# Unit 4's output products in three parts, unit 6's transposes before unit 5's scores, three weight sums moved, and all kept outputs stored ahead of unit 10's transposes

## The chip, the cores and the metric

The kernel runs on one NeuronCore of a Trainium2 chip. A time is the device time of one execution in microseconds (us). The kernel before was run three times: 223.66, 223.75 and 224.96 us, median 223.75. One further execution was taken with the hardware profiler; every duration quoted comes from it.

The core has five engines that run their own instruction streams and wait for each other by semaphores: TensorE (PE, its weight loads shown as PEld), VectorE (DVE), ScalarE (ACT), GpSimd (POOL) and SyncE (SP, which here only issues DMAs).

## What is computed

A linear-attention layer with decay, followed by a bilinear feed-forward layer. For each of 4 batches and 8 heads (sequence 768, head size 64), in blocks:

```
intra  = (q k^T * Dmask) v            Dmask[i,j] = lam^(i-j) for i >= j, else 0
inter  = (q * lam^(i+1)) kv_state
out    = intra + inter
kv_state = lam^block * kv_state + (k * lam^(block-1-j))^T v
```

The attention output, with heads side by side, is x with 3072 rows of 512. The feed-forward part has weights w_a, w_b (512 x 1536) and w_out (1536 x 512):

```
out = ((x @ w_a) * (x @ w_b)) @ w_out
```

Inputs and output are float32; the products are made in bfloat16 with float32 sums.

## The kernel before, in words

A **unit** is 128 rows of one batch for all 8 heads; there are 24, six in each batch. For a unit, q, k and v (256 KB each) are loaded by SyncE into rotating buffers (three of each, line 187). GpSimd scales k and q by powers of lam to bfloat16 (prep_k, line 401; VectorE for the first k's), and one of three engines casts v (prep_v, line 420). For units 7 to 23 SyncE then issues a transposing DMA of the scaled pair (line 429, tile qkT); for units 4 to 6 TensorE transposes it by matmuls ("T", line 443) and ScalarE copies the result (line 445). "S" makes the scores (line 457) and VectorE masks them (line 480); "V" updates the kv state (line 527) and copies it (line 560); "O" or "O2" adds inter and intra products (line 497) for one or two units and ScalarE brings the result out as xT (line 520), which is the feed-forward part's input.

The feed-forward part runs over **groups** of 4, 1, 2, 4, 4, 4, 4 and 1 units: group 0 is units 0 to 3, group 1 is unit 4 alone, group 2 is units 5 and 6, group 3 is units 7 to 10. Groups 0, 1, 2 and 7 use plain products (function ffn): for each of the 12 slices f of the inner size, a_ps and b_ps (line 596), ScalarE's cast of a_ps to a_sb (line 605) and VectorE's product ab (line 623); then per unit 12 output products op (line 643) and a store. Groups 3 to 6 (function ffn_z) use a scheme of seven products instead of eight (line 748), for which sums of the weights are made beforehand: **weight sums** 0 to 7 (function weight_sum, lines 269 to 275; even ones of w_a, odd ones of w_b; sums 6 and 7 are wz_a[3] and wz_b[3], used by the fifth product of each slice). In these groups ScalarE copies intermediate PSUM banks to tiles u of a pool of 7 buffers (snap, line 829).

**Order of the work.** Attention pieces for later units are put between the feed-forward products by hand. PLAN lists, for each group, pairs of a slot and a piece; hook(slot) issues the pieces of that slot. In ffn, slot f comes behind slice f. After the 12 slices come, for each unit t, half of the output products, slot 12 + 2t, the other half, the store, slot 13 + 2t. Within an engine the instructions run in this order; engines only wait for each other's data and buffers. Loads are issued by pump(), called at the end of prep_v and limited by a look-ahead of one to three units.

**Kept outputs.** The outputs of units 0 to 4 are copied by ScalarE (line 634) into tiles o_kept of the snap pool and not stored at once; each "W" in PLAN issues one store (store_kept, line 629), so five snap buffers stay taken until these stores have landed. Later outputs are stored at once (line 639).

All loads, transposing DMAs and stores stand in SyncE's one queue, in the order of the program. Around the change it is: transpose 7; loads of unit 10; transpose 8; kept stores 1 and 2; transposes 9 and 10; loads of units 11 and 12; transpose 11; loads of unit 13; kept store 3; transpose 12; loads of unit 14; an output; transpose 13; loads of unit 15; kept store 4; an output; kept store 5; transpose 14.

The PSUM has 7 banks in rotation for these tiles (ps_bank); a tile that comes seven later waits until the bank's reader is done.

Of the kernel before, what the change touches and what calls it, by code (L numbers as in the profile page):

```python
# [22 lines left out]
def _bc(ap, dims):  # L23
# [81 lines left out]
                        ["act"] * 3))  # L105
SUM_ENG = {(3, 0): 'dve', (3, 1): 'dve', (3, 2): 'pool', (3, 3): 'dve', (3, 4): 'pool', (3, 5): 'pool', (3, 6): 'dve', (3, 7): 'dve', (4, 0): 'dve', (4, 1): 'pool', (4, 2): 'pool', (4, 3): 'pool', (4, 4): 'dve', (4, 5): 'pool', (4, 6): 'pool', (4, 7): 'pool', (5, 0): 'dve', (5, 1): 'dve', (5, 2): 'pool', (5, 3): 'pool', (5, 4): 'dve', (5, 5): 'pool', (5, 6): 'pool', (5, 7): 'dve', (6, 0): 'pool', (6, 1): 'dve', (6, 2): 'pool', (6, 3): 'dve', (6, 4): 'dve', (6, 5): 'pool', (6, 6): 'dve', (6, 7): 'dve'}
XS_ENG = {(3, 0): 'dve', (3, 1): 'dve', (3, 2): 'dve', (4, 0): 'dve', (4, 1): 'dve', (4, 2): 'dve', (5, 0): 'dve', (5, 1): 'pool', (5, 2): 'pool', (6, 0): 'pool', (6, 1): 'pool', (6, 2): 'pool'}
WS_ENG = {0: 'dve', 1: 'dve', 2: 'dve', 3: 'dve', 4: 'dve', 5: 'dve', 6: 'dve', 7: 'pool'}
WO_ENG = {0: 'dve', 1: 'dve', 2: 'pool', 3: 'dve', 4: 'dve'}
CO_ENG = {0: 'pool', 1: 'pool', 2: 'pool', 3: 'dve', 4: 'dve', 5: 'dve'}  # L110

# [2 lines left out]
def kernel(  # L114
# [12 lines left out]
    B, H, S, D = q.shape  # L127
# [3 lines left out]
    d_model, d_ff = moe_w_a.shape  # L131
# [4 lines left out]
    FC = d_ff // 128  # L136
# [202 lines left out]
    for w, src in (("q", q), ("k", k)):  # L339
# [3 lines left out]
        for c in range(0, HP, n_c):  # L343
# [4 lines left out]
            t = t[:].rearrange("p (c b x) -> p c b x", c=n_c, b=2)  # L348
# [282 lines left out]
    def store(row, op, lo, hi, queue=None):  # L631
        if row < g_u0[KEEP_GROUPS]:
            o_sb = snap_pool.tile([128, d_model], F32, name="o_kept", tag="snap")
            nc.scalar.copy(o_sb, op)
            kept.append((row, o_sb))
            return
        o_sb = o_pool.tile([128, d_model], F32, name="o_sb", tag="osb")
        nc.scalar.copy(o_sb[:, lo:hi], op[:, lo:hi])
        (queue or nc.sync).dma_start(out=out_r[row][:, lo:hi], in_=o_sb[:, lo:hi])

    def out_mms(op, ab, t, fs, lo=0, hi=d_model):
        for f in fs:
            nc.tensor.matmul(op[:, lo:hi], lhsT=ab[:, f, t * 128:(t + 1) * 128],  # L643
                             rhs=wo_sb[:, f, lo:hi], start=(f == 0), stop=(f == FC - 1))

    def ffn(u0, n, xT, hook, first, last):
        gt = n * BLK
        ab = ab_pool.tile([128, FC, 512], BF16, name="ab", tag="ab")
        if first:
            for i, cs in enumerate(W_STEPS):  # L650
                nxt = W_STEPS[i + 1] if i + 1 < len(W_STEPS) else ()
                fs = range(w_off[cs[0]] // 128, w_off[cs[-1] + 1] // 128)
                a_sbs = a_parts(fs[:2], xT, gt) if i == 0 else []
                a_sbs += [a_part(f, xT, gt) for f in fs[len(a_sbs):]]
                if i == 0:
                    kv_update(n0 - 1)
                    cast_w("b", cs[1], "both")
                else:
                    for c in nxt:
                        cast_w("a", c, "dve")  # L660
                for n_f, (f, a_sb) in enumerate(zip(fs, a_sbs)):
                    b_part(f, xT, gt, a_sb, ab)
                    hook(f)
                    if i == 0 and n_f == 1:
                        cast_w("a", nxt[0], "dve")
                for c in nxt:
                    cast_w("b", c, "act")
            ops = [ps_bank("op", [128, d_model], F32, hold=True) for _ in range(n)]
            slot = FC
            for c in range(FC // 2):  # L670
                for t in range(n):
                    out_mms(ops[t], ab, t, range(2 * c, 2 * c + 2))
                    if c == FC // 2 - 1:
                        store(u0 + t, ops[t], 0, d_model)
                    hook(slot)
                    slot += 1
            bank["held"].clear()
            return
        for f in range(FC):
            a_sb = a_part(f, xT, gt)  # L680
            b_part(f, xT, gt, a_sb, ab)
            hook(f)
        for t in range(n):
            op = ps_bank("op", [128, d_model], F32, ffn=True)
            if last and t == n - 1:
                for lo, hi in ((0, 256), (256, 384), (384, 512)):
                    if lo:
                        op = ps_bank("op", [128, d_model], F32, ffn=True)
                    out_mms(op, ab, t, range(FC), lo, hi)
                    store(u0 + t, op, lo, hi, nc.scalar if hi == d_model else None)  # L690
                return
            out_mms(op, ab, t, range(FC // 2))
            hook(FC + 2 * t)
            out_mms(op, ab, t, range(FC // 2, FC))
            store(u0 + t, op, 0, d_model)
            hook(FC + 2 * t + 1)
# [318 lines left out]
    for g, n in enumerate(GROUPS):  # L1015
# [6 lines left out]
        def hook(slot, plan=plan):  # L1022
            for name, us in plan.get(slot, ()):
                if name == "C":
                    cast_w("o", us, CO_ENG[us])
                elif name == "PK":
                    prep_k(us)
                elif name == "PV":
                    prep_v(us)
                elif name == "P":  # L1030
                    prep_k(us)
                    prep_v(us)
                elif name == "W":
                    store_kept()
                elif name == "WS":
                    weight_sum(us)
                elif name == "WO":
                    out_sum(us)
                elif name == "SM":
                    ab_sum(*us)  # L1040
                elif name == "H":
                    out_half(*us)
                elif name == "XA":
                    x_add_first(us)
                elif name == "X":
                    x_sums(us)
                elif name == "T":
                    piece_T(us)
                elif name == "S":
                    piece_S(us)  # L1050
                elif name == "VC":
                    kv_copy(us, kv["ps"], KV_ENG[us])
                elif name == "V":
                    piece_V(us)
                elif name == "O":
                    pieces_O((us,))
                elif name == "O2":
                    pieces_O(us)
                else:
                    pieces_O(us[:2], us[2:])  # L1060
# [41 lines left out]
```

## Time and profile before

| what | value |
|---|---|
| median of three runs | 223.75 us |
| the profiled execution | 223.83 us, of which 222.1 us are the span from the first to the last instruction |
| TensorE busy | 213.9 us (96%) |
| VectorE, ScalarE, GpSimd busy | 165.3, 122.7, 99.8 us |
| bytes moved | 39.4 MB, mean 177 GB/s |
| unit 4's output products | 58.3 to 61.5 us |
| group 2's slices | 62.8 to 74.5 us |
| group 3 begins | 83.0 us |

How to read it. Times in lists are microseconds from the start of the span. A row of a timeline has the start, the duration of the whole row (several instructions may be merged, x says how many), the engine, the line, the operation, out<-in, shapes and, in brackets, how long the engine had been idle and what ended that. "SPq" rows are SyncE issuing a DMA: their duration is that of the issue, and the transfer lands some microseconds later. Matmuls are pipelined, so a busy TensorE says only that something was in its pipe; gaps are found from the distance of one matmul's start to the next. An idle time of an engine that is not the bottleneck costs nothing by itself.

### The profile page before, as it was taken

The numbers are of one execution on the slowest core, as the hardware profiler recorded it, in microseconds if no ns is written. First come the engines' busy times: TensorE is split into PE (matmuls) and PEld (weight loads), VectorE is DVE, ScalarE is ACT, GpSimd is POOL, SyncE is SP. The second block draws the span as 40 slices with busy tenths as digits, with TensorE's granted clock in tenths as the row PEclk, the third lists the DMA queues.
The fourth block names the chain that finished last, engine by engine and source line by source line (L and its number), as shares of the span: only waits on it lengthen the run. The fifth ranks groups of instructions, "written<-read, shape, count | busy, mean of one in ns | idle before, by whom it ended". The sixth has DMA issues, their size and how long they took to land.

```text
span 222.1 us, 5601 instructions
## 1 busy us (share of the span) xinstructions
PE 213.9 (96%) x2225; PEld 159.0 (72%) x2235; DVE 165.3 (74%) x272; ACT 122.7 (55%) x249; POOL 99.8 (45%) x95
## 2 busy tenths in 40 slices
PE   7899999999999999999999999899999999999994
PEld 2476444448678657787547888688888888888994
DVE  0994773968798668889888889968688865777540
ACT  3686446038454266775356988776535666543322
POOL 6061004246795175540559559786417722051100
PEclk9999999999999999999999999999999999999999
DMA  4999999999999999999999999652021100112042
GB/s 132 321 265 349 356 387 344 277 216 218 216 204 220 232 174 248 190 275 245 180 248 236 233 201 211 138 101 50 0 88 56 52 0 4 47 47 97 0 145 94
DMA packets 99081, 39.42 MB, mean 177 GB/s; under 512 B 85488, under 2 KB 95088, under 8 KB 99056
## 3 DMA queue, kind: packets, MB, share of 16 engines
q1 hardware_dynamic: 98768, 39.00, 79.8%
q8 instruction: 17, 0.28, 0.6%
q10 hardware_dynamic: 288, 0.07, 0.1%
q14 instruction: 8, 0.07, 0.1%
HBM read 28.32 MB, written 6.29 MB: 156 GB/s over the span
## 4 chain that ended last, share of the span: by engine, by line
PE 67%; DMA 16%; SPq 5%; DVE 5%; ACT 2%; issue 2%; POOL 1%; ACTq 0%; DVEq 0%; POOLq 0%
PE U L748 17%; PE op L870 12%; PE V L748 9%; DMA wst<-in_moe_w_b_dram 8%; PE b_ps L596 5%; PE op L810 5%; PE a_ps L596 5%; PE W L748 4%; PE op L643 3%; DMA kf<-in_k_dram 3%; DMA k<-in_k_dram 3%; PE o_ps L497 3%; PE kq L457 2%; DMA out_dram<-o_kept 2%; SPq L187 1%
## 5 line engine op out<-in xcount | busy, mean ns | idle before, releaser
L829 ACT COPY u<-U 128x512 f32<-128x512 f32 x48 | 28.3, 590 | 16.5 <-PE U L748 16.4
L401 POOL TENSOR_TENSOR qk<-kf,lp_k 128x512 bf16<-128x512 f32 x18 | 19.5, 1084 | 33.7 <-DMA kf<-in_k_dram 18.9
L623 DVE TENSOR_TENSOR ab<-a_sb,b_ps 128x128 bf16<-128x128 bf16 (+2 forms) x48 | 19.2, 417 | 13.6 <-ACT a_sb L605 10.2
L596 PE MATMUL a_ps<-xT,wa_sb 128*128 128x128 bf16 (+2 forms) x198 | 27.6, 267 | 0.5 <-DVE wa_sb L244 0.2
L480 DVE TENSOR_TENSOR m<-kq,lotri 128x512 bf16<-128x512 f32 x40 | 25.6, 682 | 3.1 <-PE kq L457 3.0
L596 PE MATMUL b_ps<-xT,wb_sb 128*128 128x128 bf16 (+2 forms) x192 | 27.5, 272 | 0.2
L756 DVE TENSOR_TENSOR ab<-oab 128x1024 bf16<-128x1024 bf16 x24 | 19.0, 791 | 11.3 <-ACT oab L754 11.1
L401 POOL TENSOR_TENSOR qk<-qf,lp_q 128x512 bf16<-128x512 f32 x20 | 24.8, 1242 | 1.7 <-DMA qf<-in_q_dram 1.7
L605 ACT CAST a_sb<-a_ps 128x128 bf16<-128x128 f32 (+2 forms) x48 | 17.3, 374 | 14.7 <-PE a_ps L596 14.4
L643 PE MATMUL op<-wo_sb,ab 128*128 128x512 bf16 (+2 forms) x114 | 21.8, 334 | 0.5 <-issue 0.3
L596 PEld LDWEIGHTS <-wa_sb 128*128 128x128 bf16 x200 | 16.7, 98 | 6.6 <-issue 0.5
L748 PEld LDWEIGHTS <-wz_a 128*128 128x128 bf16 x192 | 18.2, 98 | 3.9 <-issue 0.9
L748 PEld LDWEIGHTS <-wz_b 128*128 128x128 bf16 x192 | 18.7, 98 | 2.2
L596 PEld LDWEIGHTS <-wb_sb 128*128 128x128 bf16 x192 | 15.8, 98 | 6.2 <-issue 0.2
L748 PE MATMUL U<-xT,wz_a 128*128 128x256 bf16 x96 | 18.3, 272 | 0.0
L748 PE MATMUL U<-xT,wz_b 128*128 128x256 bf16 x96 | 18.3, 272 | 0.0
L520 ACT CAST xT<-o_ps 128x512 bf16<-128x512 f32 (+1 forms) x24 | 12.2, 554 | 10.7 <-PE o_ps L497 10.5
L787 DVE TENSOR_TENSOR oab<-U,u 128x512 bf16<-128x512 f32 x24 | 16.3, 681 | 0.8 <-PE U L748 0.8
L420 POOL CAST vb<-vf 128x512 bf16<-128x512 f32 x14 | 10.2, 730 | 13.8 <-DMA vf<-in_v_dram 13.8
L748 PEld LDWEIGHTS <-wa_sb 128*128 128x128 bf16 x144 | 13.4, 98 | 4.0 <-issue 1.0
L643 PEld LDWEIGHTS <-ab 128*128 128x128 bf16 x120 | 10.1, 98 | 8.5
L754 ACT CAST oab<-U 128x512 bf16<-128x512 f32 x24 | 14.2, 592 | 3.5 <-PE U L748 3.5
(130 smaller groups left out, 453.1 us busy)
## 6 DMA issues: line engine op xcount, KB each, us to landing
vf<-in_v_dram SPq DMA_DIRECT2D x24, 256.0 KB, 4.9
qf<-in_q_dram SPq DMA_DIRECT2D x20, 256.0 KB, 4.6
kf<-in_k_dram SPq DMA_DIRECT2D x20, 256.0 KB, 4.7
out_dram<-o_sb SPq DMA_DIRECT2D x18, 256.0 KB, 2.4
wst<-in_moe_w_a_dram SPq DMA_DIRECT2D x6, 512.0 KB, 8.8
wst<-in_moe_w_b_dram SPq DMA_DIRECT2D x6, 512.0 KB, 9.2
wst<-in_moe_w_out_dram SPq DMA_DIRECT2D x6, 512.0 KB, 10.7
out_dram<-o_kept SPq DMA_DIRECT2D x5, 256.0 KB, 4.3
```

The costliest lines, as they stand in the source:

```text
L401: eng_of(eng).tensor_mul(dst.rearrange("p (c b) d -> p b c d", b=2), x[:].rearrange("p (b c) d -> p b c d", b=2), lp.rearrange("p (b c) o ...
L480: nc.vector.tensor_mul(m, kq[i], lotri_bc)
L596: nc.tensor.matmul(ps[:, lo:hi], lhsT=w_sb[:, s, f * 128:(f + 1) * 128], rhs=xT[:, s, lo:hi], start=(s == 0), stop=(s == KS - 1), skip_gro ...
L605: nc.scalar.copy(a_sb[:, :gt], ps[:, :gt])
L623: nc.vector.tensor_mul(ab[:, f, :gt], a_sb[:, :gt], ps[:, :gt])
L643: nc.tensor.matmul(op[:, lo:hi], lhsT=ab[:, f, t * 128:(t + 1) * 128], rhs=wo_sb[:, f, lo:hi], start=(f == 0), stop=(f == FC - 1))
L748: nc.tensor.matmul(ps[:, k, :], lhsT=wt[:, s, n * 128:(n + 1) * 128], rhs=rhs[i][:, s, :], start=(fresh and k == 0 and s == 0), stop=True, ...
L754: nc.scalar.copy(oab[:, 0], U)
L756: nc.vector.tensor_mul(ab[:].rearrange("p (h i) (t c) -> p h i t c", h=2, t=2)[:, :, n], o5[:, :, :, 0, :], o5[:, :, :, 1, :])
L787: nc.vector.tensor_sub(oab[:, 1], U, v1)
L829: nc.scalar.copy(t, ps)
L870: nc.tensor.matmul(ps[:, t, :], lhsT=lhs[p][:, n, t * 128:(t + 1) * 128], rhs=rhs[:, n, :], start=fresh, stop=True, skip_group_check=True)
```

## The change

Four things are edited.

1. Unit 4's output products (the branch n == 1 of ffn, which only group 1 takes): 4 products, slot 12, 4 products, slot 13, 4 products, store. Before: 6 products, slot 12, 6 products, store, slot 13. So the pieces of slot 13 (preparation of unit 8, O2 of units 5 and 6, V of unit 6 and a weight sum) stand ahead of the last 4 products, and ScalarE's copy of unit 4's output behind its copies of xT.
2. At slot 11 of group 1, T of unit 6 comes before S of unit 5.
3. Weight sum 5 goes from slot 0 to slot 13 of group 1. Sum 6 goes from slot 13 of group 1 to slot 9 of group 2. Sum 7 goes from slot 13 of group 1 to slot 13 of group 2, and from GpSimd to VectorE. VectorE has one instruction more, GpSimd one less.
4. The kept stores: three at slot 2 of group 2 (before: two), two at slot 6 (before: one each at slots 11, 13 and 15). In SyncE's queue, store 3 now stands ahead of transpose 9 and stores 4 and 5 between transposes 9 and 10; the later places are empty. The number of DMAs is the same.

TensorE has the same instructions. Its order changes only at unit 5's scores and unit 6's transposes, and in the place of the output products of unit 4.

```diff
-    1: [(0, 'PV', 5), (0, 'WS', 5), (3, 'T', 5), (4, 'PK', 6), (6, 'PV', 6), (9, 'P', 7),
-        (11, 'S', 5), (11, 'T', 6), (12, 'S', 6), (13, 'P', 8), (13, 'O2', (5, 6)), (13, 'V', 6),
-        (13, 'WS', 6), (13, 'WS', 7)],
-    2: [(2, 'W', None), (2, 'W', None), (3, 'P', 9), (4, 'V', 7), (4, 'S', 7),
-        (6, 'V', 8), (10, 'PK', 10), (11, 'PV', 10), (11, 'P', 11), (11, 'W', None),
+    1: [(0, 'PV', 5), (3, 'T', 5), (4, 'PK', 6), (6, 'PV', 6), (9, 'P', 7),
+        (11, 'T', 6), (11, 'S', 5), (12, 'S', 6), (13, 'P', 8), (13, 'O2', (5, 6)), (13, 'V', 6), (13, 'WS', 5)],
+    2: [(2, 'W', None), (2, 'W', None), (2, 'W', None), (3, 'P', 9), (4, 'V', 7), (4, 'S', 7),
+        (6, 'V', 8), (6, 'W', None), (6, 'W', None), (9, 'WS', 6), (10, 'PK', 10), (11, 'PV', 10), (11, 'P', 11),
         (11, 'S', 8), (11, 'P', 12), (12, 'Q', (7, 8, 9, 10)), (13, 'P', 13),
-        (13, 'W', None), (13, 'V', 9), (14, 'XA', 3), (14, 'O2', (9, 10)), (14, 'X', 3), (15, 'W', None)],
+        (13, 'V', 9), (13, 'WS', 7), (14, 'XA', 3), (14, 'O2', (9, 10)), (14, 'X', 3)],
...
-WS_ENG = {0: 'dve', 1: 'dve', 2: 'dve', 3: 'dve', 4: 'dve', 5: 'dve', 6: 'dve', 7: 'pool'}
+WS_ENG = {0: 'dve', 1: 'dve', 2: 'dve', 3: 'dve', 4: 'dve', 5: 'dve', 6: 'dve', 7: 'dve'}
...
+            if n == 1:
+                out_mms(op, ab, t, range(4))
+                hook(FC)
+                out_mms(op, ab, t, range(4, 8))
+                hook(FC + 1)
+                out_mms(op, ab, t, range(8, FC))
+                store(u0 + t, op, 0, d_model)
+                return
             out_mms(op, ab, t, range(FC // 2))
             hook(FC + 2 * t)
             out_mms(op, ab, t, range(FC // 2, FC))
```

## The prediction

> **What bounds the kernel.** First the page: the share of each engine, then the clock and DMA rows.
>
> ```profile
> PE 213.9 (96%) x2225; PEld 159.0 (72%) x2235; DVE 165.3 (74%) x272; ACT 122.7 (55%) x249; POOL 99.8 (45%) x95
> ...
> PEclk9999999999999999999999999999999999999999
> DMA  4999999999999999999999999652021100112042
> ```
>
> TensorE is busy 96% of the span at full clock, so its work sets the time and the only prize is a gap in it. The DMA engines are full until slice 25 (139 us), so in the stretch of the change (51 to 97 us) a transfer put forward puts others back. Second, the TensorE timeline, compared with an even stream: between 51 and 97 us I find four real gaps. At 54.13 us 0.27 us; at 62.80 and 63.29 us 0.29 and 0.27; at 88.75 us 0.51 (start-to-start excess over the 0.11 us of a 256-column matmul). Excesses of about 0.22 us elsewhere are a 512-column matmul missing from the trace (groups of 5 where 6 were issued). Together 1.34 us, 0.6% of the span: the change can win no more. Third, the timelines of the engines that end these gaps:
>
> ```profile
> 52.48 1.39 DVE L273 TENSOR_TENSOR wz_b<-wb_sb,wz_b 128x1536 bf16<-128x1536 bf16 x1
> 53.80 0.67 DVE L623 TENSOR_TENSOR ab<-a_sb,b_ps 128x128 bf16<-128x128 bf16 x3
> ...
> 61.39 2.70 DVE L420 CAST vb<-vf 128x512 bf16<-128x512 f32 x1
> ```
> ```profile
> 61.58 0.58 ACT L634 COPY o_kept<-op 128x512 f32<-128x512 f32 x1 [2.01 <-PE op L643]
> 62.17 1.07 ACT L520 CAST xT<-o_ps 128x512 bf16<-128x512 f32 x2
> ```
> ```profile
> 84.85 0.40 PE L457 MATMUL kq<-qkT 64*128 64x128 bf16 x8
> ...
> 88.75 0.38 PE L748 MATMUL V<-z_add,wz_a 128*128 128x256 bf16 x2 [0.34 <-ACT u L829]
> ```
>
> Weight sum 5 holds VectorE for 1.39 us, the products behind it start at 53.80, and their PSUM banks come free late: gap one. ScalarE copies unit 4's output before it brings xT out, and the next group needs xT: gaps two and three. Before 88.75 ScalarE's copy u had waited 0.8 us for the landing of the third kept store (the only wait on such a store in the list of waits), whose buffer it reuses: gap four.
>
> Fourth, SyncE's queue and GpSimd, since transposes are issued there:
>
> ```profile
> 67.21 1.35 SPq L629 DMA_DIRECT2D out_dram<-o_kept  x2
> 68.74 3.20 SPq L429 DMA_TRANSPOSE qkT<-qk  x2
> 72.00 0.57 SPq L187 DMA_DIRECT2D qf<-in_q_dram  x1
> 72.62 0.58 SPq L187 DMA_DIRECT2D kf<-in_k_dram  x1
> ...
> 79.26 2.08 SPq L429 DMA_TRANSPOSE qkT<-qk  x1
> ...
> 83.72 1.03 SPq L629 DMA_DIRECT2D out_dram<-o_kept  x1
> ```
> ```profile
> 53.02 1.75 POOL L401 TENSOR_TENSOR qk<-qf,lp_q 128x512 bf16<-128x512 f32 x1
> ...
> 60.71 3.09 POOL L275 TENSOR_TENSOR wz_b<-wb_sb 128x1536 bf16<-128x1536 bf16 x1
> ...
> 77.19 1.04 POOL L401 TENSOR_TENSOR qk<-kf,lp_k 128x512 bf16<-128x512 f32 x1 [6.84 <-PE o_ps L497]
> 78.19 1.04 POOL L401 TENSOR_TENSOR qk<-qf,lp_q 128x512 bf16<-128x512 f32 x1
> ```
>
> SyncE issues without a pause from 60 to 78 us. Unit 11's k load is issued at 72.62 and lands 4.41 us later, at 77.03; GpSimd scales it 0.16 us after that (the releaser printed is another semaphore of the same moment), then q to 79.2; the transpose of unit 11 goes out at 79.26, takes 4.96 us, lands at 84.22, and TensorE reads it in the score matmuls at 84.85. This chain has 84.85 - 84.22 - 0.15 = **0.48 us to spare**. Unit 12's transpose lands at 89.0 for scores at 89.77; units 9, 10, 13 and 14 have 2 us or more.
>
> **The change, part by part**, against the profiled execution's 223.83 us (span 222.1; median of the runs 223.75, so the same).
>
> 1. Weight sum 5 from slot 0 of group 1 to its end: gap one goes, -0.27. At its new place (VectorE after unit 6's state copy) it takes the place of sum 6, same shape (0.95 to 1.39 against 1.19), in front of group 2's first product. Cover: the cast in front of it loses GpSimd's neighbour (part 3), so VectorE arrives earlier than before.
> 2. Unit 6's transposes (8) before unit 5's scores (8), output products 4+4+4. ScalarE's copy of the transposes takes 1.01 us (58.56) and unit 6's scores wait for it. Between the two stood 6 matmuls of 0.22 = 1.31 us; now 8 score matmuls (0.33) and 4 products (0.87) = 1.20, against 0.22 + 1.01 + 0.17 = 1.40 needed: +0.2. At the end the copy of xT no longer stands behind the copy of the output, and 4 products (0.87 us) lie between xT's source and its first reader: -0.56. The output copy now stands before group 2's first a_sb copy and frees the bank of its second a_ps at about the moment it is wanted: 0 to +0.1. Parts 1 and 2 together: **-0.66**.
> 3. Sum 7 from GpSimd (3.09 us) to VectorE at slot 13 of group 2 (0.95), sum 6 to slot 9. Sum 6 fits in VectorE's four pauses of 0.45 us per product there. Sum 7 falls at about 79.5, ahead of z_add (80.06), in the 1.6 us in which VectorE waits for xT: 0 on VectorE. Its cost is on GpSimd: beside sum 5 the q scaling took 1.75 us instead of 1.04, beside sum 6 again 1.75. Delayed as in part 4, unit 11's q scaling runs about 79.6 to 80.7, on top of sum 7. Bounds 0 and +0.95 (all of sum 7); I take the row, +0.71, in the chain that has 0.48 to spare. Freeing GpSimd at 60.7 brings unit 9 forward, which nothing waits for.
> 4. Kept stores 3, 4, 5 from after unit 13's and 15's loads to before unit 9's transpose (one) and unit 10's (two): on SyncE ahead of two transposes and the loads of units 11 and 12. Issuing one costs 0.36 to 0.49 us plus 0.06 between (the 67.21 pair), three 1.25 to 1.65; in landings, each spaces the queue by 0.64 to 0.72, three 2.0, less a pause of 0.7 (unit 10's transpose landed at 73.96, q of unit 11 1.86 later, where loads follow each other at 1.17). Both ways k of unit 11 is **1.25 to 1.65 later; I take 1.45**. Bounds: 0 (all in pauses) and 3.3 (three at 1.03 + 0.06, as the third was held at 83.72). Gap four goes, -0.51, as all kept stores land by 76 us.
>
> At unit 11's scores: its transpose is issued at 79.26 + 1.45 + 0.71 = 81.42. Its latency is 4.96 in place, 4.2 for units 8 and 12; I take 4.6: landing 86.02, scores 86.17. TensorE, early by 0.66, would be there at 84.2 and waits 2 us, with all of group 3 queued behind; parts 1 and 2 are swallowed whole. Against 84.85 that is +1.32. From there -0.51 for gap four; unit 12's transpose, no longer behind a store, lands near 90.05, before its scores at 90.1 to 90.6. Sum: +0.81, **224.6 us**. Own range: with 1.25, no neighbour, 4.2 it is 223.3; with 1.65, 0.95, 4.96 it is 225.4.
>
> The Trainium skill, "SBUF — State Buffer", section "Who interferes with whom", makes the port that VectorE and GpSimd share an exclusive lock: of a VectorE operation with two SBUF inputs and a GpSimd one that reads, the second fully blocks. The 2.70 us cast (0.56 at 57.06) agrees: it ends 0.3 us after GpSimd's 3.09 us operation. It speaks against part 3; its result is rival three.
> The Trainium skill, "DMA: Bandwidth & Descriptors", section "Queues, rings and completion order", says that each DMA engine takes one queue's descriptors in ring order, which speaks against part 4; the landings come in order of issue here too, and by it the 2.0 us would be paid except for pauses.
>
> **Rivals.**
> - *The gain is kept* (0.23). The stores fill pauses: before the first kept store landed there was a pause too (2.15 us after unit 8's transpose, 1.5 more than a store's spacing). With 0 delay and no neighbour, unit 11 lands at 84.22, scores 84.37: -0.48 - 0.51 = **222.8**; with the neighbour 223.5. Against: SyncE itself has no pause there.
> - *Slower for good* (0.12). SyncE is held 1.09 us by each of the three stores: 3.3 us, scores at 87.67: +2.82 - 0.51 = **226.1**. The change loses as soon as the chain is over 1.0 us late. For: the store at 83.72. Against: the pair at 67.21.
> - *Full blocking* (0.10). The q scaling of unit 11 stands behind sum 7 and z_add, 0.95 + 0.41 = 1.36 instead of 0.71: **225.3**. For: the cast of 2.70. Against: sum 5 and its neighbour both went on, longer.
> - *The store's wait stays* (0.05): the buffer at 88.1 is held by another user; +0.51, **225.1**.
> - Forecast: 0.50.
>
> **Numbers.** 1% (2.2 us: 221.6 and 226.1) is about what a measurement of this kernel tells from no change. Faster by more needs more than all gaps: 0.02. Slower by more: half of the second rival and a tail of the forecast, 0.08. The range 222.6 to 226.0 goes from the kept gain to that bound.
>
> **What the profile will show.** Right: no gaps at 54 and 62 to 63, group 2 some 0.7 us earlier; the cast of 2.70 back at 0.5; unit 11's k load issued at 73.3 to 73.7; a q scaling near 1.75 beside sum 7; TensorE waiting 1 to 2 us for unit 11's transpose; no wait of u on a kept store. Wrong: if unit 11's scores start before 84.85, the stores were free; if unit 12's scores wait as well, the loss is larger.

## The result

The changed kernel took 225.53 us (median of 18 runs, 223.93 to 227.68), the kernel before, beside it on the same chip, 224.14 us (18 runs, 223.41 to 225.45). The ratio, **1.0043 with a 95% interval of 1.0022 to 1.0064**, leaves out disturbed runs and so is less than that of the two medians: slower by 0.96 us on 224.14 (0.5 to 1.4), which is clear of zero and within the 1% that the prediction took as no change. The forecast was 224.6 us against 223.83; 223.75 times the ratio is 224.7.

The profiled execution of the changed kernel took 225.28 us (span 223.6). Its start-up, in which nothing was changed, was 0.32 us longer: unit 4's scores start at 48.36 us, against 48.04 before. Times of after are therefore compared with before less 0.32. A DMA has landed when its semaphore says so in the trace. Line numbers of after are one lower from L48 on, and 7 higher in ffn_z and behind it (L748 and L829 of before are L755 and L836).

The shares of the engines, from the page of after:

```profile
PE 213.7 (96%) x2225; PEld 159.0 (71%) x2235; DVE 164.3 (73%) x273; ACT 122.6 (55%) x249; POOL 96.1 (43%) x94
```

TensorE's work is the same; the difference lies in its gaps. Its timeline, the scores of units 10 to 12 (columns as in the lists above):

```profile
76.60 0.40 PE L456 MATMUL kq<-qkT 64*128 64x128 bf16 x8 [0.39 <-DMA qkT<-qk]
...
85.75 0.40 PE L456 MATMUL kq<-qkT 64*128 64x128 bf16 x8 [0.73 <-DMA qkT<-qk]
90.68 0.40 PE L456 MATMUL kq<-qkT 64*128 64x128 bf16 x8 [0.49 <-DMA qkT<-qk]
```

All four gaps of before are gone, and three new ones stand in their place, each a wait for a transpose at scores: unit 10's at 76.60, unit 11's at 85.75, unit 12's at 90.68. Start to start they cost 0.55, 0.89 and 0.66 us. Ahead of them the gain can still be seen: unit 7's scores, in the middle of group 2, start at 67.31, which less the 0.32 is 0.77 us sooner than before (67.76).

VectorE's timeline, where before had the sum of 1.39 us and the cast of 2.70 us:

```profile
61.34 0.43 DVE L419 CAST vb<-vf 128x512 bf16<-128x512 f32 x1 [0.20 <-DMA vf<-in_v_dram]
...
62.56 0.95 DVE L272 TENSOR_TENSOR wz_b<-wb_sb,wz_b 128x1536 bf16<-128x1536 bf16 x1
...
72.84 0.95 DVE L274 TENSOR_TENSOR wz_a<-wa_sb 128x1536 bf16<-128x1536 bf16 x1
...
80.18 1.83 DVE L274 TENSOR_TENSOR wz_b<-wb_sb 128x1536 bf16<-128x1536 bf16 x1
```

Sums 5 and 6 take 0.95 us, the cast 0.43. Sum 7, at 80.18, takes 1.83. GpSimd's timeline beside it:

```profile
79.15 1.04 POOL L400 TENSOR_TENSOR qk<-kf,lp_k 128x512 bf16<-128x512 f32 x1 [8.42 <-DMA kf<-in_k_dram]
80.15 1.04 POOL L400 TENSOR_TENSOR qk<-qf,lp_q 128x512 bf16<-128x512 f32 x1
81.14 1.34 POOL L419 CAST vb<-vf 128x512 bf16<-128x512 f32 x1
```

Unit 11's q scaling (80.15) took its usual 1.04 us, not the 1.75 that the prediction gave it: the price of the meeting fell on sum 7. ScalarE's timeline, where the copy of unit 4's output stood ahead of xT:

```profile
61.41 1.07 ACT L519 CAST xT<-o_ps 128x512 bf16<-128x512 f32 x2 [2.17 <-PE o_ps L496]
62.82 0.59 ACT L633 COPY o_kept<-op 128x512 f32<-128x512 f32 x1 [0.34 <-PE op L642]
```

xT now comes first. SyncE's queue, in the stretch of the stores:

```profile
67.43 1.84 SPq L628 DMA_DIRECT2D out_dram<-o_kept  x3
69.45 1.70 SPq L428 DMA_TRANSPOSE qkT<-qk  x1
71.20 1.05 SPq L628 DMA_DIRECT2D out_dram<-o_kept  x2
72.36 1.34 SPq L428 DMA_TRANSPOSE qkT<-qk  x1
73.75 0.57 SPq L186 DMA_DIRECT2D qf<-in_q_dram  x1
74.37 0.86 SPq L186 DMA_DIRECT2D kf<-in_k_dram  x1
...
81.22 2.38 SPq L428 DMA_TRANSPOSE qkT<-qk  x1
```

Unit 11's k load is issued at 74.37 (72.62 before, so 1.43 later) and lands at 78.99 (77.03, so 1.64 later). Unit 12's k load, two loads further back, lands at 83.86 instead of 80.58: 2.96 later. The chain of waits, followed to unit 12's scores, shows it as the longest piece (the last experiment asks whether this chain is what held the transpose):

```profile
77.41 6.45 DMA kf<-in_k_dram
...
84.02 0.85 POOL qk L400
...
85.02 1.04 POOL qk L400
86.06 0.40 POOL vb L419
86.47 4.16 DMA qkT<-qk
...
90.68 0.40 PE kq L456 x8
```

From unit 11's scores on, the change stays 0.58 to 0.69 us behind (unit 14's scores 105.06 against 104.05, less 0.32: 0.69), and so at the last scores. The other 0.45 us or so by which this one execution is longer lies behind the last matmul, in a stretch that differs from 3.14 to 3.62 us between the profiles of all kernels here.

### The profile page after: what moved, and what is told of

It reads as the page before. It is cut to its first block, busy times and chain, and to the rows that moved or that the text cites. A ratio compares the mean times of both kernels' runs of the same rounds, so it can differ in the third digit from the quotient of the medians.

```text
span 223.6 us, 5597 instructions
## 1 busy us (share of the span) xinstructions
PE 213.7 (96%) x2225; PEld 159.0 (71%) x2235; DVE 164.3 (73%) x273; ACT 122.6 (55%) x249; POOL 96.1 (43%) x94
## 4 chain that ended last, share of the span: by engine, by line
PE 78%; DMA 11%; DVE 4%; SPq 2%; POOL 1%; issue 1%; ACT 1%; DVEq 0%; ACTq 0%; POOLq 0%
PE U L755 17%; PE op L877 12%; PE b_ps L595 10%; PE a_ps L595 9%; PE V L755 9%; DMA kf<-in_k_dram 6%; PE op L817 5%; PE W L755 4%; PE o_ps L496 4%; PE op L642 3%; DMA k<-in_k_dram 3%; PE kq L456 2%; DMA qkT<-qk 2%; PE kvd L526 2%; SPq L349 1%; DVE m L479 1%
## 5 line engine op out<-in xcount | busy, mean ns | idle before, releaser
L836 ACT COPY u<-U 128x512 f32<-128x512 f32 x48 | 28.3, 590 | 17.0 <-PE U L755 16.9
L400 POOL TENSOR_TENSOR qk<-qf,lp_q 128x512 bf16<-128x512 f32 x20 | 23.4, 1169 | 1.6 <-DMA qf<-in_q_dram 1.6
L755 PEld LDWEIGHTS <-wz_a 128*128 128x128 bf16 x192 | 18.2, 98 | 3.4 <-issue 0.2
L755 PEld LDWEIGHTS <-wz_b 128*128 128x128 bf16 x192 | 18.8, 98 | 2.2
L755 PE MATMUL U<-xT,wz_a 128*128 128x256 bf16 x96 | 18.3, 272 | 0.0
L755 PE MATMUL U<-xT,wz_b 128*128 128x256 bf16 x96 | 18.3, 272 | 0.0
L755 PEld LDWEIGHTS <-wa_sb 128*128 128x128 bf16 x144 | 13.5, 98 | 4.0 <-issue 1.0
```

The source lines that it names most:

```text
L400: eng_of(eng).tensor_mul(dst.rearrange("p (c b) d -> p b c d", b=2), x[:].rearrange("p (b c) d -> p b c d", b=2), lp.rearrange("p (b c) o ...
L755: nc.tensor.matmul(ps[:, k, :], lhsT=wt[:, s, n * 128:(n + 1) * 128], rhs=rhs[i][:, s, :], start=(fresh and k == 0 and s == 0), stop=True, ...
L836: nc.scalar.copy(t, ps)
```

## The experiments

All but "part 4 alone" keep parts 1 to 3 and differ from the change in the stores or in one other thing. The table gives the ratio to the kernel before with its interval, and from the profiled execution the distance from unit 7's to unit 14's scores (parts 1 to 3 lie ahead of it, the stores in it; 36.29 us in before) and the gaps of TensorE in that distance that end with a transpose or a kept store, start to start.

| kernel | ratio | unit 7 to 14 | gaps |
|---|---|---|---|
| stores 3 to 5 left out | 0.996 [0.994, 0.998] | 36.04 | unit 12: 0.30 |
| late stores, q first | 0.9976 [0.995, 1.0002] | 36.29 | unit 12: 0.65 |
| stores 4, 5 at group 3, slot 11 | 0.998 [0.9959, 1.0] | 36.48 | unit 12: 0.83 |
| stores 4, 5 at group 3, slot 15 | 0.9997 [0.9974, 1.0019] | 36.66 | unit 12: 1.02 |
| only store 3 early | 1.0019 [0.9994, 1.0044] | 36.76 | unit 12: 0.31; store 4: 0.76 |
| part 4 undone | 0.9994 [0.9971, 1.0018] | 37.07 | unit 11: 0.27; store 3: 1.12 |
| stores 4, 5 at slot 12 | 1.0028 [1.0001, 1.0054] | 37.21 | unit 12: 0.65; store 4: 0.63 |
| part 4 alone | 1.0071 [1.0044, 1.0097] | 37.54 | units 11, 12: 0.89, 0.77 |
| sum 7 at slot 9 | 1.0045 [1.0016, 1.0073] | 37.58 | units 10, 11, 12: 0.43, 0.88, 0.63 |
| the change | 1.0043 [1.0022, 1.0064] | 37.75 | units 10, 11, 12: 0.55, 0.89, 0.66 |
| five stores first | 1.0056 [1.0028, 1.0084] | 38.29 | units 10, 11, 12: 0.60, 0.85, 0.90 |
| stores 4, 5 by ScalarE | 1.0033 [1.0007, 1.0058] | 38.47 | units 10, 11, 12: 1.53, 0.47, 0.67 |
| the change, q first | 1.0255 [1.0217, 1.0294] | 38.50 | units 10, 11: 0.60, 1.74; and see there |

### Part 4 undone

```diff
-    2: [(2, 'W', None), (2, 'W', None), (2, 'W', None), (3, 'P', 9), ...
-        (6, 'V', 8), (6, 'W', None), (6, 'W', None), (9, 'WS', 6), ... (11, 'P', 11),
+    2: [(2, 'W', None), (2, 'W', None), (3, 'P', 9), ...
+        (6, 'V', 8), (9, 'WS', 6), ... (11, 'P', 11), (11, 'W', None),
...
+        (13, 'W', None), (13, 'V', 9), ... (15, 'W', None)],
```

> The changed kernel with part 4 undone: the kept stores stand where the kernel before has them, parts 1 to 3 stay. Theory (the stores ahead of unit 11's loads make the loss): unit 11's transpose lands near 84.2 us again, TensorE is there at about the same moment and waits 0 to 0.3 us; the wait for the third kept store comes back, at the same absolute time (88.0 us), and so is longer than before (0.9 to 1.0 us instead of 0.51). Parts 1 and 2 show in the trace as group 2 starting 0.7 us earlier and are lost at that wait: the time is that of the kernel before, within 0.3 us (ratio 0.998 to 1.002). Rival (the new order in group 1 or the sums on VectorE make the loss): it stays slow, ratio near 1.004.

Ratio 0.9994 [0.9971, 1.0018]: parts 1 to 3 alone are worth nothing that can be measured. They bring TensorE to group 3 sooner, but the third store is where it was, so ScalarE's copy u waits longer for it (ScalarE's timeline of this kernel):

```profile
89.14 0.58 ACT L836 COPY u<-V 128x512 f32<-128x512 f32 x1 [1.44 <-DMA out_dram<-o_kept]
```

1.44 us instead of 0.83, and TensorE's gap behind it is 1.12 instead of 0.51. Most of the gain is given back at the next thing that a DMA sets: less the start-up this kernel is 1.08 us ahead of before at unit 7's scores and 0.30 at unit 12's.

### Part 4 alone

```diff
 # the kernel before, with
+    2: [(2, 'W', None), (2, 'W', None), (2, 'W', None), (3, 'P', 9), ...
+        (6, 'V', 8), (6, 'W', None), (6, 'W', None), (10, 'PK', 10), ...
```

> The kernel before with part 4 alone. Theory: unit 11's loads are late by the same 1.5 to 2 us, TensorE waits about 0.9 us at unit 11's scores and up to 0.7 us at unit 12's, the wait for the third kept store is gone: as slow as the changed kernel, ratio 1.003 to 1.006, though parts 1 to 3 are missing. Rival: without parts 1 to 3 there is only the gain of the kept store's wait, ratio near 0.998.

Ratio 1.0071 [1.0044, 1.0097], a little more than expected, with the waits at the scores of units 11 and 12 (0.89 and 0.77 us) and the gap at 54.63 us (0.38) still there. The loss of the change comes from part 4. Its interval overlaps that of the whole change, so how much of it parts 1 to 3 take back isn't told by the two ratios.

### Only the third store put forward

```diff
-        (6, 'V', 8), (6, 'W', None), (6, 'W', None), (9, 'WS', 6), ...
+        (6, 'V', 8), (9, 'WS', 6), ...
...
+        (13, 'W', None), (13, 'V', 9), ... (15, 'W', None)],
```

> The changed kernel with only the third kept store ahead of unit 9's transpose; the fourth and fifth stand where the kernel before has them. Theory: one store puts unit 11's loads back by 0.4 to 0.7 us, its transpose lands at 84.6 to 84.9, TensorE waits 0.5 to 0.8 us there, which swallows parts 1 and 2, but the wait for the third store (0.51 us) is gone and unit 12's transpose is no later than before: 0.3 to 0.6 us faster than the kernel before (ratio 0.997 to 0.999). Rival: as slow as the changed kernel, 1.004.

The time missed: 1.0019 [0.9994, 1.0044]. The waits at the scores of units 10 and 11 are gone, though 0.5 to 0.8 us had been expected at unit 11's, and that at unit 12's is down to 0.31. But store 4, issued behind unit 13's transpose and unit 15's loads, is now itself late (ScalarE's timeline of this kernel):

```profile
99.89 0.58 ACT L836 COPY u<-U 128x512 f32<-128x512 f32 x1 [1.41 <-DMA out_dram<-o_kept]
```

Store 4 lands at 99.82, and TensorE loses 0.76 us there. In before the same store did no harm: ScalarE came to its wait for it one copy u later, at 100.20, when the store had landed (99.78).

### Stores 3 to 5 left out

```diff
-    2: [(2, 'W', None), (2, 'W', None), (2, 'W', None), (3, 'P', 9), ...
-        (6, 'V', 8), (6, 'W', None), (6, 'W', None), (9, 'WS', 6), ...
+    2: [(2, 'W', None), (2, 'W', None), (3, 'P', 9), ...
+        (6, 'V', 8), (9, 'WS', 6), ...
```

> The changed kernel with kept stores 3, 4 and 5 left out altogether: the output rows of units 2, 3 and 4 are not written; every computation stays. Theory: unit 11's transpose lands at 84.2 as in the kernel before, unit 12's earlier (88.4), no wait on a kept store: the gain of all parts is seen, 0.9 to 1.1 us faster than the kernel before (ratio 0.995 to 0.996). Rival (parts 1 to 3 make the loss): ratio near 1.002 to 1.004.

0.996 [0.994, 0.998], 0.9 us under the kernel before: all gains show when nothing has to be paid for the stores. No place of the stores that was tried comes below it, and the change lies 1.9 us above it.

### Stores 4 and 5 behind the loads of unit 14

```diff
-        (6, 'V', 8), (6, 'W', None), (6, 'W', None), (9, 'WS', 6), ...
-        (11, 'S', 8), (11, 'P', 12), (12, 'Q', (7, 8, 9, 10)), ...
+        (6, 'V', 8), (9, 'WS', 6), ...
+        (11, 'S', 8), (11, 'P', 12), (12, 'W', None), (12, 'W', None), (12, 'Q', (7, 8, 9, 10)), ...
```

> The changed kernel with kept stores 4 and 5 moved from slot 6 to slot 12 of group 2: behind the loads and transposes of units 11 and 12 and the loads of unit 14, ahead of unit 13's transpose. Theory (the loss is what stands ahead of the loads of units 11 and 12; the cost of late stores is a buffer wanted at 88 and at 100 us): units 11 and 12 are as in the run with the third store alone put forward (no wait at their scores), stores 4 and 5 land near 94 us, before ScalarE wants their buffers at 98 to 100 us, and unit 13's transpose, some 1.3 us later, has 2.7 us to spare. All gains stay: ratio to the kernel before 0.995 to 0.997, about 223.2 us, faster than both kernels. Rival (another limit appears wherever the two stores go, because the DMA engines are full): a wait of 0.4 us or more at the scores of unit 12 or 13 or at a copy u, ratio 0.999 or more.

The rival was right: 1.0028 [1.0001, 1.0054]. Unit 11's scores don't wait, but two other limits appear (ScalarE's and TensorE's timelines of this kernel):

```profile
95.16 0.58 ACT L836 COPY u<-U 128x512 f32<-128x512 f32 x1 [0.57 <-DMA out_dram<-o_kept]
```

```profile
89.33 0.40 PE L456 MATMUL kq<-qkT 64*128 64x128 bf16 x8 [0.48 <-DMA qkT<-qk]
...
95.79 0.38 PE L755 MATMUL U<-z_mix,wz_a 128*128 128x256 bf16 x2 [0.46 <-ACT u L836]
```

Which copy u takes which free buffer is fixed when the kernel is built, and follows from where the stores stand: put forward by a slot, store 4's buffer goes to the copy at 95 us, not to one at 98 to 100. It landed at 95.08, half a microsecond too late. The expectation had reckoned with the old order.

### All five stores first

```diff
-    2: [(2, 'W', None), (2, 'W', None), (2, 'W', None), (3, 'P', 9), ...
-        (6, 'V', 8), (6, 'W', None), (6, 'W', None), (9, 'WS', 6), ...
+    2: [(2, 'W', None), (2, 'W', None), (2, 'W', None), (2, 'W', None), (2, 'W', None), (3, 'P', 9), ...
+        (6, 'V', 8), (9, 'WS', 6), ...
```

> The changed kernel with all five kept stores at slot 2 of group 2, so stores 4 and 5 stand ahead of unit 9's transpose instead of between those of units 9 and 10. Theory (what counts is how many stores stand ahead of the loads of units 11 and 12, and not where): unit 11's k load lands as late as in the changed kernel, TensorE waits 0.7 to 0.9 us at unit 11's scores and some 0.5 us at unit 12's, ratio to the kernel before 1.003 to 1.006. Rival (the place between two transposes is what costs, because the DMA engines pause there in any case or pause once more): the wait at unit 11's scores is under 0.3 us, ratio 0.998 to 1.001. New in either case: unit 9's transpose is about 1.3 us later, with 2 us to spare.

1.0056 [1.0028, 1.0084], waits of 0.85 and 0.90 us: the place of stores 4 and 5 between two transposes is not what costs, their number ahead of the loads is. The other profiles agree: unit 11's transpose lands, less each one's start-up, at 82.9 to 84.2 us with none of stores 3 to 5 ahead of its loads, at 83.5 to 84.2 with one and at 84.9 to 86.2 with all three, so the first of them costs it nothing that shows. This run also tells how VectorE and GpSimd hold each other up. VectorE's and GpSimd's timelines of this kernel:

```profile
80.22 1.68 DVE L274 TENSOR_TENSOR wz_b<-wb_sb 128x1536 bf16<-128x1536 bf16 x1
```

```profile
80.05 1.04 POOL L400 TENSOR_TENSOR qk<-kf,lp_k 128x512 bf16<-128x512 f32 x1 [9.12 <-DMA kf<-in_k_dram]
81.05 1.76 POOL L400 TENSOR_TENSOR qk<-qf,lp_q 128x512 bf16<-128x512 f32 x1
```

Here the q scaling does take 1.76 us. Sum 7 starts at 80.22, while the k scaling runs; if it stands still until that ends at 81.09 and then needs 0.81, it ends at 81.90, as it does. The q scaling, issued at 81.05, stands still until 81.90 and then needs 0.91: 82.81. In the changed kernel the order was the other way: q at 80.15, sum 7 at 80.18, and sum 7 stands still until 81.19 (plus 0.82 gives 82.01, its end); the v cast of 81.14 waits for that and ends at 82.48. The 1.39 and 1.75 of the kernel before come out in the same way: GpSimd's k scaling ends at 53.06, sum 5 0.81 later at 53.87, the q scaling 0.90 after that, at 54.77; and so does the 1.75 beside sum 6 (k scaling to 64.99, sum 6 to 65.80, q scaling to 66.70). In none of these rows do the two run together: who comes second waits for the whole of the other, and who waits goes next. This is the rule of the Trainium skill, "SBUF — State Buffer", section "Who interferes with whom", which adds that the order of issue decides who blocks; these rows agree.

### Stores 4 and 5 from ScalarE's queue

```diff
-        nc.sync.dma_start(out=out_r[row], in_=o_sb)
+        queue = nc.scalar if row >= 3 else nc.sync
+        queue.dma_start(out=out_r[row], in_=o_sb)
```

> The changed kernel with kept stores 4 and 5 issued from ScalarE instead of SyncE, at the same places of the program. SyncE's queue then has the loads of units 11 and 12 one step of 1.1 us sooner, while the same bytes go through the same DMA engines. Theory A (the time SyncE needs to issue the two stores, 0.5 us each, is what delays unit 11's and 12's loads): their loads and transposes are as in the run with the third store alone put forward, no waits at the scores of units 11 and 12, ratio to the kernel before 0.996 to 0.999. Theory B (the transfers, 0.65 us each, are what delays): the loads land as late as in the changed kernel, waits of 0.5 us or more stay, ratio 1.002 to 1.006.

1.0033 [1.0007, 1.0058], as theory B expected. Unit 11's k load was issued at 74.11 and landed at 79.63; less the start-up, 0.21 us shorter here, that is 0.05 us sooner than in the changed kernel and 0.85 later. SyncE no longer spends 1.05 us on the two stores, but its other issues took longer by as much (unit 10's transpose 1.86 us instead of 1.34, unit 11's q load 1.26 instead of 0.57), so freeing it helped nothing. That fits theory B; that the DMA engines hold the transfers, and not SyncE's queue, is argued here and not shown by itself. Worse, unit 10's transpose, issued at 70.89, landed at 77.56 (in the changed kernel issued at 72.36, landed at 76.55). The fifth store, which ScalarE issued 0.94 us behind it, landed 0.19 us ahead of it, and unit 10's scores (TensorE's timeline of this kernel) waited longest:

```profile
77.61 0.40 PE L456 MATMUL kq<-qkT 64*128 64x128 bf16 x8 [1.37 <-DMA qkT<-qk]
```

### Sum 7 away from unit 11's scaling

```diff
-        ... (9, 'WS', 6), (10, 'PK', 10), ...
-        (13, 'V', 9), (13, 'WS', 7), ...
+        ... (9, 'WS', 6), (9, 'WS', 7), (10, 'PK', 10), ...
+        (13, 'V', 9), ...
```

> The changed kernel with weight sum 7 at slot 9 of group 2, beside sum 6, instead of slot 13, so VectorE is not busy with it while GpSimd scales unit 11's q. As predicted (a sum beside it makes that scaling 0.71 us longer): unit 11's transpose is issued 0.7 us sooner, TensorE's wait there goes, ratio to the kernel before about 1.001. Theory by the trace after (that scaling took 1.04 us beside sum 7, as alone, and sum 7 itself took 1.83 instead of 0.95): unit 11's transpose is issued where it was, ratio 1.003 to 1.006, and sum 7 takes 0.95 to 1.4 us.

1.0045 [1.0016, 1.0073], unit 11's wait 0.88 as in the change: sum 7 at its place cost nothing. At slot 9, with no neighbour, it took 0.95 us. The q scaling took 1.22 us here, behind another operation of VectorE.

### Stores 4 and 5 in group 3

Two places: behind unit 14's and behind unit 15's transpose.

```diff
-        (6, 'V', 8), (6, 'W', None), (6, 'W', None), (9, 'WS', 6), ...
+        (6, 'V', 8), (9, 'WS', 6), ...
 # the one
+    3: [... (10, 'P', 14), (11, 'W', None), (11, 'W', None), (12, 'S', 13),
 # the other
+        (15, 'P', 15), (15, 'W', None), (15, 'W', None), ...
```

The later place (slot 15):

> The changed kernel with the third kept store at slot 2 of group 2 as it is, and stores 4 and 5 moved from slot 6 of group 2 to slot 15 of group 3, behind unit 15's transpose and the loads after it. Their two snap buffers are then wanted only in group 4 (the order in which ScalarE's copies u wait for stores is fixed when the kernel is built: with the stores in group 2 a copy u at 95 or 100 us waits for store 4, here none of group 3 does). Theory (the loss lies in what stands ahead of the loads of units 11 and 12, and in a late store whose buffer is wanted): no wait over 0.3 us at the scores of units 10 to 15, none at a copy u; all gains of the other parts stay: ratio to the kernel before 0.995 to 0.998, near the run without stores 3 to 5, some 1.5 us below the changed kernel, faster than both. Rival (with the DMA engines full until 139 us the two stores cost their 1.3 us wherever they go): a wait of 0.4 us or more at unit 16's to 18's scores, ratio 0.999 or more.

The earlier one (slot 11):

> As the run before, with stores 4 and 5 at slot 11 of group 3, behind unit 14's transpose and the loads after it, so unit 15's transpose is the one that they push back by some 1.3 us; in the run with the third store alone put forward it landed at 108.1 for scores at 111.6. Theory: no wait there either, ratio 0.995 to 0.998. Rival: a wait at unit 15's scores or at a copy u, ratio 0.999 or more.

0.9997 [0.9974, 1.0019] and 0.998 [0.9959, 1.0]; the first misses the 0.995 to 0.998 expected of it, the second is at its edge, and the two can't be told apart. No scores of units 10, 11 or 13 to 18 wait and no copy u in group 3: the stores cost nothing there. What is left is unit 12's wait, which was expected under 0.3 and is 1.02 and 0.83 (TensorE's timeline with the stores at slot 11):

```profile
84.39 0.40 PE L456 MATMUL kq<-qkT 64*128 64x128 bf16 x8
89.49 0.40 PE L456 MATMUL kq<-qkT 64*128 64x128 bf16 x8 [0.66 <-DMA qkT<-qk]
```

TensorE, no longer stopped by anything before, meets unit 12's transpose, which lands at 89.44. Against the changed kernel this version is faster (the intervals don't touch); that it beats the kernel before lies at the edge of its interval.

### q scaled before k

```diff
-        make_ks(u, "dve" if u < n0 + 2 else "pool")
-        make_qs(u, "pool")
+        if u >= 11:
+            make_qk_q_first(u)        # the same two scalings, q's first
+        else:
+            make_ks(u, "dve" if u < n0 + 2 else "pool")
+            make_qs(u, "pool")
```

In the changed kernel:

> The changed kernel with one thing more: from unit 11 on GpSimd scales q before k. The q of a unit lands 1.1 us ahead of its k, so its scaling (1.04 us) then lies beside k's transfer instead of behind k's scaling. Theory (TensorE's waits in the changed kernel hang on the chain from the landing of k over the scalings and the transpose): the transposes of units 11 and 12 are issued about 1.0 us sooner, at 80.2 and 85.4; the wait at unit 11's scores goes (landing 84.7, TensorE there at 84.9), that at unit 12's stays at some 0.6 us, because TensorE comes there 0.9 us sooner; ratio to the kernel before about 1.000, 0.9 us below the changed kernel. Rival (the transposes land no sooner, because SyncE or the DMA engines hold them behind the loads of unit 12 and 13): waits and ratio (1.003 to 1.006) as in the changed kernel.

In the kernel with stores 4 and 5 at group 3, slot 11:

> The kernel with the third store early and stores 4 and 5 at slot 11 of group 3 (0.998 of the kernel before, its only remaining wait in the stretch 0.83 us at unit 12's scores), with q scaled before k from unit 11 on. Theory: unit 12's transpose is issued at 84.0 instead of 85.0 and lands at 88.4, ahead of its scores; no wait over 0.3 us from 50 to 110 us; ratio to the kernel before 0.993 to 0.996, 222.6 to 223.2 us, faster than both kernels. Rival (the transpose is held behind unit 13's loads): ratio as without, 0.997 to 0.999.

Both missed. SyncE's timeline of the second, and of the same kernel without it (L428 is L437 with the new function in):

```profile
78.64 3.53 SPq L437 DMA_TRANSPOSE qkT<-qk  x1
...
84.16 2.98 SPq L437 DMA_TRANSPOSE qkT<-qk  x1
```

```profile
79.91 2.18 SPq L428 DMA_TRANSPOSE qkT<-qk  x1
...
84.97 2.42 SPq L428 DMA_TRANSPOSE qkT<-qk  x1
```

Unit 11's transpose is issued 1.27 us sooner, but its issue takes 1.35 longer, and it lands at 84.21 instead of 84.10; unit 12's is issued 0.81 sooner and lands 0.19 sooner. Waiting for the scalings is not what held them. In all fourteen profiles unit 12's transpose lands 0.83 to 0.97 us behind the DMA ahead of it in the queue, whenever it is issued; unit 11's lands 0.84 to 0.94 behind unit 12's v load in ten of them, the changed kernel among them (85.71 after 84.80). Only in before and in the run with part 4 undone (1.65 and 1.64), with five stores first (1.19, issued later) and with the change and q first (1.52, SyncE held 2.51 us by the v load ahead) was it later. So in the changed kernel the transposes wait for what stands in the DMA engines ahead of them; for that kernel itself these distances are the evidence, since with q first in it the transpose was issued no sooner (82.03 against 81.22, with a start-up 0.56 us longer).

The second kernel's ratio is hardly better than without q first (0.9976 and 0.998), though unit 12's wait fell from 0.83 to 0.65, since the new order meets VectorE elsewhere. Unit 15's scores come 0.66 us later behind unit 14's (8.08 us, without it 7.42). GpSimd's and VectorE's timelines of this kernel:

```profile
103.42 1.04 POOL L400 TENSOR_TENSOR qk<-qf,lp_q 128x512 bf16<-128x512 f32 x1 [3.90 <-DMA qf<-in_q_dram]
```

```profile
103.48 1.53 DVE L772 TENSOR_TENSOR ab<-oab 128x1024 bf16<-128x1024 bf16 x1 [0.17 <-ACT oab L770]
```

The product ab, issued 0.06 us behind the q scaling, stands still until that ends at 104.46 and takes 1.53 us instead of 0.69.

The change with q first took 229.83 us, 2.55% or 5.7 us more than before. Up to unit 14's scores it is only 1.13 us behind before; the main loss is at 123.68 us, in a stretch that the change doesn't touch. TensorE's, VectorE's and GpSimd's timelines of this kernel:

```profile
123.68 0.39 PE L764 MATMUL U<-z_mix,wz_a 128*128 128x256 bf16 x2 [2.61 <-DVE z_mix L742]
```

```profile
120.33 3.30 DVE L742 TENSOR_TENSOR z_mix<-xT 128x512 bf16<-128x512 bf16 x1
```

```profile
119.82 3.52 POOL L289 TENSOR_TENSOR wy<-wo_sb 128x1536 bf16<-128x1536 bf16 x1
```

z_mix stands still until GpSimd's weight sum ends at 123.34, then needs 0.29. In the changed kernel z_mix was issued at 117.90 and that sum at 119.60: 1.70 us of distance; with late stores and q first 117.94 and 118.45, so 0.51. Here it is 0.51 the other way: against the changed kernel z_mix came 2.43 us later and the sum 0.22. Which of the shifts ahead of it turned the order over wasn't taken apart. And the gap costs more than itself. The windows of this kernel around it (columns: stretch, its length, then busy time and instructions of PE, PEld, DVE, ACT and POOL, the granted clock, DMA share, GB/s):

```profile
121.00:125.00 4.00, 1.38 (x14) 1.05 (x14) 4.00 (x4) 0.67 (x2) 4.00 (x3) 1.00 1.23 179
125.00:128.00 3.00, 3.00 (x20) 1.92 (x19) 1.71 (x3) 1.46 (x4) 1.29 (x2) 0.51 1.34 232
128.00:131.00 3.00, 3.00 (x59) 2.32 (x56) 2.63 (x4) 2.42 (x6) 1.69 (x3) 0.92 0.78 218
```

By these windows the granted clock fell to half at about 125.05, 1.4 us after TensorE took up work again, for some 3.4 us. From unit 16's to unit 17's scores it is 7.44 us here and 3.45 in the changed kernel: 2.78 for the gap, 1.2 for the clock by then. That is read from this one execution: four of the kernel's six runs show a mean granted clock of 0.992 or 0.993, the other two 1.0, and these two (228.73 and 230.68 us) are no shorter. The Trainium skill, "TensorE: Matmul & The Clock Gate", Part 1, says that the clock is halved after an idle window of about 3.4 us; here an idle time of 2.61 was enough, and the measurement decides.

## Why the prediction was right, and where it was not

The forecast, 224.6 us against 223.83, so +0.8, met the ratio's +0.96, inside its interval (+0.5 to +1.4). Its main line held, that the gain of parts 1 and 2 would be swallowed at scores that wait for a transpose, made late by part 4. Two of its terms were wrong, unit 11's scores 0.74 us too late and a wait of 0.66 us at unit 12's that it didn't have. They nearly cancel: the direction and its cause were foreseen, but that the number is so close is luck.

- **Parts 1 and 2, -0.66**: unit 7's scores came 0.77 sooner (0.40 to 1.08 in the other profiles with these parts). Right in size, though the terms listed there add up to -0.63 to -0.53; the new wait of 0.2 that was counted at unit 6's scores didn't show as a gap. They were swallowed as said: without the stores 0.9 us show, with them nothing.
- **Part 4, k of unit 11 1.45 later**: 1.43 in its issue, 1.64 in its landing, the end of its range. Right. (The pair's row of 1.35 holds 0.50 us between the two issues, not the 0.06 that was read; the three stores put forward took 1.84 - 1.35 + 1.05 = 1.54 us of SyncE.)
- **Sum 7 beside unit 11's q scaling, +0.71: wrong.** The scaling took 1.04, and moving the sum away changed nothing. The rows of before were read as two operations that slow each other down, and full blocking was put at 0.10 with those rows against it. They were rows of blocking, with a chain of three operations in it: k scaling, sum, q scaling. (The cast of 2.70 us waits in the same way, but it reads one tile, and so is no case of the two SBUF inputs of the rule beside which it was put.) With blocking it matters who comes first, and q came first, by 0.03 us. The price was paid by sum 7 and the v cast (1.83 and 1.34 us), both off the path. Had sum 7 come first, it would have been 0.72 (the five stores first); even there unit 11's wait was no longer than in the change, as the transpose landed 3.16 us after its late issue.
- **Unit 11's transpose, latency 4.6, landing 86.02**: issued at 80.90 and landed at 85.39 (less 0.32), so 4.49. The 0.63 us by which the forecast was late come in the main from the 0.71. But the form of the term, an issue and a latency, was not what held it: its landing follows that of unit 12's v load by 0.9.
- **Gap four, -0.51**: the wait of u on a store is gone. Right. Part 4 undone brings it back, at 1.12.
- **Unit 12's transpose lands before its scores: wrong.** Predicted 90.05, it came at 90.31 (less 0.32), and TensorE, at unit 11's scores 0.74 sooner than predicted, waited 0.66. This takes back what gap four gave: from unit 11's to unit 12's scores it is 4.93 us after and 4.92 before. The step that failed is "no longer behind a store". It stood behind the loads of units 12 and 13, and these were late by the stores (unit 12's k load by 2.96, of which the forecast worked out only unit 11's 1.64). In before, the long distance between two landings of this stretch, 1.99 us, fell behind unit 12's k (80.58 to 82.57); after, one of 2.61 us falls ahead of its q (80.19 to 82.80), and so ahead of its k too.
- Of the **rivals**, *the gain is kept* fell with the 1.43 us of the issue; *slower for good* supposed 1.09 us of SyncE for each store, where three took 1.84 and two 1.05 together; *the store's wait stays* did not happen here, though the runs with one store early and with stores at slot 12 showed its mechanism one store further on. *Full blocking* had the mechanism right and the order of issue wrong, so its time was not put to the test.
- Of the **signs**, three came: no gaps at 54 and 62 to 63, the short cast, no wait on a store. Unit 11's q scaling didn't lengthen. The issue of its k load, 74.05 less the start-up, is outside the 73.3 to 73.7 given for it, which doesn't fit the prediction's own 72.62 + 1.45 either; the wait at unit 11 is 0.89 and not 1 to 2 us, since its scores came 0.74 us sooner than forecast and unit 10's wait had held TensorE up before. Unit 12's scores do wait, the sign of a larger loss, and the loss isn't larger, because TensorE had lost 0.74 us less at unit 11's.

Unit 10's wait of 0.55 us was not in the forecast at all. By this account it costs nothing by itself, since TensorE would have waited for unit 11 in its place; no run takes it out alone.

## What to carry to other kernels

Where the DMA engines are full, transfers put forward are paid for by what stands behind them in the queue, first of all by loads that the bounding engine will wait for. Here one store ahead of unit 11's loads cost nothing that shows, and three put its transpose back by 0.7 to 2 us against before; what is not urgent belongs behind these loads, at a place with slack. A gain ahead of such a point is given back there, so look for the next thing that a DMA sets before adding up gaps. And before a longer row is read as "both slow down", put the starts and ends of both engines side by side: here each pair looked at came out as the second waiting for the whole of the first.

## What the runs showed of the hardware that was not expected

- In every row looked at VectorE's sums of SBUF tiles and GpSimd's scalings exclude each other completely, and the order of issue decides: the same scaling took 1.04 us when it came 0.03 us ahead of the sum, and 1.76 when the sum was already waiting. Far from the change, an order turned over by half a microsecond made an operation of 1.26 us in the changed kernel take 3.30.
- A transpose issued 1.27 us sooner into a full queue landed no sooner (84.21 instead of 84.10): its issue took 3.53 instead of 2.18 us.
- With two stores on ScalarE's queue, one that was issued 0.94 us behind a transpose of SyncE's landed 0.19 us ahead of it. Unit 10's scores waited 1.53 us instead of 0.55, and the loads landed no sooner.
- An idle time of 2.61 us was enough for the granted clock of TensorE to fall to 0.51, not at once but 1.4 us after work was taken up, so in this execution a single gap of 2.78 us cost about 4.
